# The inverse of steps 0 and 1 from products on TensorE, and groups of four from step 2 on, in a DeltaNet and MLP kernel

## Chip, cores and metric

One core of a Trainium2 chip. The metric is the device time of one execution in microseconds (us); the median of four executions is quoted (of seven for the kernel before). A "span" is the time of the one profiled execution from its first to its last record; it is 1.7 us below the run's own time in the runs before and after.

## The reference

A DeltaNet recurrence on 4 batches, 8 heads, 768 tokens and 48 features, then an MLP with a hard-swish on the 3072 x 384 result.

```python
k_n = k / (norm(k) + 1e-6)
for t in range(S):
    y[t]  = q[t] @ state
    state = state + beta[t] * outer(k_n[t], v[t] - k_n[t] @ state)
x = y as (B*S, H*D)                 # 3072 x 384
h = x @ w_in                        # 384 -> 2048
out = (h * clip(h + 3, 0, 6) / 6) @ w_out
```

`w_in` and `w_out` come as 64-bit floats and are converted to FP32 on the chip, in 16 pieces of 768 KB.

## The kernel before

The sequence is cut into 24 steps of 32 tokens. In a step, all heads of all batches are worked at once, and the recurrence inside the step becomes the inverse of a unit triangular 32x32 matrix for each of 32 heads and batches. `prep` makes k, q (transposed) and the matrix L of a step; `inverse` inverts L for four steps at once on VectorE; `chain` carries the state; `up` and `down` are the MLP.

```python
def prep(t, dma):                   # cut
    kb  = kf * inv                  # GpSimd
    mb  = beta * mask               # GpSimd
    bkb = kb * beta                 # GpSimd
    yield
    KQ  = transposes of kb, qb      # TensorE pt, ScalarE
    sc  = KQ products               # TensorE
    LB  = sc * mb                   # VectorE
    l_dram[g][i] <- L               # DMA

def inverse(g, dma, back):          # cut
    A <- l_dram[g]                  # 4 steps x 8 heads x 4 batches on 128 partitions
    for j in range(1, C - 1):       # 30 steps, each waits for the one before
        pr = A[:, j, j+1:] * A[:, 0:j, j]
        A[:, 0:j, j+1:] -= pr
        yield
    x_dram[g] <- A                  # DMA
    LB <- x_dram[g]                 # DMA, 4 of them

def convert():                      # cut: 5 instructions on VectorE, 1 on ScalarE per piece

for t in range(CB, N):              # cut: the main loop, 16 MLP units beside each chain
    ch = chain(t)
    for u in range(16):
        ...                         # a part of the chain, of a prep
        take(conv, 2)               # two of the five parts of a conversion
        take(units)
        take(fill, 1 + (u % 2 == 0))    # norms and inverse of later groups
```

The order of every engine's queue is written by hand in the program. (A few names below are short for those of the kernel: `kf` is raw k, `inv` the inverse of its norm, `R` and `Z` are steps of the chain on VectorE and ScalarE.)

## Time and profile before

| | kernel before |
|---|---|
| time, median of 7 executions (third batch) | 779.2 us (777.5 to 780.9) |
| span of the profiled execution | 777.2 us |
| first pz (chain of step 0) | 84.6 us |
| first ph (MLP) | 106.3 us |
| ks of step 4, of step 5, of step 6 | 155.4, 203.6, 231.9 us |
| granted TensorE clock, mean | 0.953 |

pz, ks, py and su are the products of the chain of a step, ph and po those of the MLP, pt and sc those of prep; g is VectorE's part of the hard-swish. "ks of step n" is the place where step n begins.

### The profile page before, as it was taken

Reading aid. Unit: us, or ns where it says so; the run is one execution under the profiler, and the core shown is the slowest. Engines: PE = TensorE matmul, PEld = TensorE weight load, DVE = VectorE, ACT = ScalarE, POOL = GpSimd, SP = SyncE. Lnnn points to the kernel's source line nnn. Section 1 sums busy time; section 2 is a strip of 40 time slices with the busy share of each in tenths; the row PEclk is TensorE's granted clock in tenths of the full one; section 3 lists DMA queues with packets and bytes.
Section 4 is the critical chain, followed back from the end, with each engine's and each line's share of the span. In section 5 each row is a group of like instructions: output and inputs, shape, how many; then the busy total and the mean of one; then the engine's idle time right before and its main releaser. Section 6 shows DMA issues by size and latency. Waiting matters only on the chain.

```text
span 777.2 us, 24923 instructions
## 1 busy us (share of the span) xinstructions
PE 677.8 (87%) x11208; PEld 500.1 (64%) x11208; DVE 356.2 (46%) x868; ACT 178.8 (23%) x354; POOL 92.0 (12%) x139
## 2 busy tenths in 40 slices
PE   1441587558799999999999999999999999999997
PEld 1330465446576776876876867867868768677674
DVE  6269859968527731247711367511464213021020
ACT  1211221222321231321322311313213113122120
POOL 4451021003004002012011040020000000000000
PEclk9995569889999999999999999999999999999999
DMA  5771750356311131330142501311103010000000
GB/s 101 184 148 48 168 115 32 116 133 187 70 39 50 23 77 35 73 65 17 44 67 45 90 29 25 66 26 30 48 12 82 6 30 3 13 13 0 21 1 20
DMA packets 140139, 45.77 MB, mean 59 GB/s; under 512 B 130272, under 2 KB 133344, under 8 KB 140032
## 3 DMA queue, kind: packets, MB, share of 16 engines
q1 hardware_dynamic: 131312, 42.23, 23.9%
q10 hardware_dynamic: 8720, 1.93, 1.3%
q8 instruction: 88, 1.44, 0.8%
q14 instruction: 19, 0.16, 0.1%
HBM read 33.13 MB, written 11.01 MB: 57 GB/s over the span
## 4 chain that ended last, share of the span: by engine, by line
PE 76%; DVE 12%; issue 3%; DMA 3%; POOL 3%; SPq 1%; ACT 1%; POOLq 0%; DVEq 0%; ACTq 0%
PE po L480 32%; PE ph L459 30%; DVE A L323 3%; DVE pr L319 3%; PE pz L371 2%; PE py L371 2%; PE su L428 2%; PE sc L287 2%; PE pt L274 2%; PE ks L361 2%; PE py L361 2%; DMA kf<-in_k_dram 1%; DMA d<-in_moe_w_in_dram 1%; DVE e L184 1%; DVE m L180 1%
## 5 line engine op out<-in xcount | busy, mean ns | idle before, releaser
L459 PE MATMUL ph<-xT,w_in 128*128 128x256 f32 x1152 | 273.8, 390 | 18.1 <-DVE w_in L189 10.2
L480 PE MATMUL po<-w_out,g 128*128 128x384 f32 x768 | 265.1, 494 | 4.0 <-DVE w_out L189 4.0
L459 PEld LDWEIGHTS ph<-xT,w_in 128*128 128x128 f32 x1152 | 216.5, 193 | 52.0 <-DVE w_in L189 10.6
L480 PEld LDWEIGHTS po<-w_out,g 128*128 128x128 f32 x768 | 141.6, 191 | 90.5 <-issue 5.6
L468 DVE SCALAR_TENSOR_TENSOR g<-t,ph 128x256 f32<-128x256 f32 x192 | 80.5, 419 | 188.6 <-ACT t L464 188.3
L464 ACT ACTIVATE t<-ph,halves 128x256 f32<-128x256 f32 x192 | 90.9, 474 | 194.1 <-PE ph L459 183.0
L323 DVE TENSOR_TENSOR A<-A,pr 128x30 f32<-128x30 f32 (+9 forms) x180 | 68.0, 378 | 6.2
L319 DVE TENSOR_TENSOR pr<-A 128x30 f32<-128x30 f32 (+9 forms) x180 | 66.8, 371 | 4.3
L436 DVE TENSOR_TENSOR state<-state,su 128x384 f32<-128x384 f32 x46 | 23.3, 547 | 67.9 <-PE su L428 67.9
L277 ACT ACTIVATE KQ<-pt 128x512 f32<-128x512 f32 x48 | 28.3, 595 | 83.6 <-PE pt L274 80.5
L287 PE MATMUL sc<-KQ 64*32 64x64 f32 x1536 | 23.1, 255 | 27.6 <-ACT KQ L277 27.6
L274 PE MATMUL pt<-ident,kb 128*128 128x128 f32 x96 | 18.1, 320 | 32.9 <-POOL kb L252 32.9
L293 DVE TENSOR_TENSOR LB<-sc,mb 128x512 f32<-128x512 f32 x24 | 16.5, 688 | 61.9 <-PE sc L287 58.4
L259 POOL TENSOR_TENSOR mb<-beta_tok,mask 128x256 f32<-128x256 f32 x48 | 32.0, 687 | 82.8 <-DVE LB L293 82.8
L252 POOL TENSOR_TENSOR kb<-kf,inv 128x384 f32<-128x384 f32 x24 | 20.7, 863 | 160.7 <-PE pt L274 131.7
L287 PEld LDWEIGHTS sc<-KQ 64*32 64x32 f32 x1536 | 18.8, 120 | 31.4 <-ACT KQ L277 30.3
L210 POOL TENSOR_TENSOR sq<-kf 128x384 f32<-128x384 f32 x21 | 17.4, 827 | 182.5 <-DMA kf<-in_k_dram 104.3
L274 PEld LDWEIGHTS pt<-ident,kb 128*128 128x128 f32 x96 | 13.4, 163 | 37.9 <-POOL kb L252 34.0
L486 ACT ACTIVATE o<-po 128x384 f32<-128x384 f32 x24 | 11.8, 491 | 111.5 <-PE po L480 111.5
L170 ACT ACTIVATE e<-e,rebias 128x768 uint32<-128x768 uint32 x16 | 15.0, 936 | 83.8 <-DVE e L169 83.7
L387 DVE TENSOR_TENSOR R<-vf,ks 128x384 f32<-128x384 f32 x23 | 12.7, 550 | 37.2 <-PE ks L361 37.2
L371 PEld LDWEIGHTS py<-Z,LB 32*32 32x32 f32 x1536 | 19.1, 109 | 13.7 <-issue 11.8
(56 smaller groups left out, 397.6 us busy)
## 6 DMA issues: line engine op xcount, KB each, us to landing
d<-in_moe_w_in_dram SPq DMA_DIRECT2D x8, 768.0 KB, 6.0
d<-in_moe_w_out_dram SPq DMA_DIRECT2D x8, 768.0 KB, 5.7
kf<-in_k_dram SPq DMA_DIRECT2D x96, 48.0 KB, 2.5
vf<-in_v_dram SPq DMA_DIRECT2D x96, 48.0 KB, 2.2
out_dram<-o SPq DMA_DIRECT2D x96, 48.0 KB, 1.6
qb<-in_q_dram SPq DMA_DIRECT2D x80, 48.0 KB, 2.4
x_dram<-A SPq DMA_DIRECT2D x6, 512.0 KB, 2.9
LB<-x_dram SPq DMA_DIRECT2D x24, 128.0 KB, 2.9
```

Source lines behind the costliest of these rows:

```text
L259: nc.gpsimd.tensor_tensor(out=mb[:, e], in0=beta_tok[:, t, e:H:2].unsqueeze(2).unsqueeze(3).to_broadcast([P, NP, 2, C]), in1=mask2[:].unsq ...
L274: nc.tensor.transpose(pt[:, p, :], src[:, 2 * p : 2 * p + 2].rearrange("p e w -> p (e w)"), ident[:])
L277: nc.scalar.activation(out=KQ[:, :, j, :], in_=pt[:], func=ACTF.Copy)
L287: nc.tensor.matmul(scv[rows(b), e, p], lhsT=KQ[r, p, 0, rows(b)], rhs=KQ[r, p, :, rows(b)], start=True, stop=True,)
L319: nc.vector.tensor_tensor(out=pv, in0=A[:, j, j + 1 :].unsqueeze(1).to_broadcast([128, j, n]), in1=A[:, 0:j, j].unsqueeze(2).to_broadcast( ...
L323: nc.vector.tensor_tensor(out=A[:, 0:j, j + 1 :], in0=A[:, 0:j, j + 1 :], in1=pv, op=ALU.subtract)
L361: nc.tensor.matmul(ph[rows(b), e, D * p : D * p + D], lhsT=KQ[r, p, j, rows(b)], rhs=state[r, b, p, :], start=(p == 0), stop=True, skip_gr ...
L371: nc.tensor.matmul(place(h, b), lhsT=m(h)[rows(b)], rhs=z[rows(b), D * h : D * h + D], start=start, stop=True, skip_group_check=True, tile ...
L459: nc.tensor.matmul(ph[:], lhsT=w_in[:, s, f * 128 : (f + 1) * 128], rhs=xT[:, s, :], start=(s == 0), stop=(s == NKT - 1),)
L464: nc.scalar.activation(out=t1[:], in_=ph[:], func=ACTF.Relu, bias=half, scale=1.0 / 6.0)
L468: nc.vector.scalar_tensor_tensor(out=g[:], in0=t1[:], scalar=1.0, in1=ph[:], op0=ALU.min, op1=ALU.mult)
L480: nc.tensor.matmul(po[:], lhsT=gs[blk, f][:, c * P : (c + 1) * P], rhs=w_out[:, f, :], start=(f == 0), stop=(f == NFC - 1),)
```

## The change

Steps 0 and 1 should not wait for the serial inverse and its way through DRAM. They become a group of their own, whose inverse comes from six rounds of 32x32 products on TensorE per step, with transposes on VectorE between them. The serial inverse then serves groups of steps 2 to 5, 6 to 9 and so on, the last with two steps. The order of the first steps is written anew around this, k and raw weights get separate buffers, and bkb is made later.

```diff
+    NG = 1 - (CB - N) // GS
+    def group(t):
+        return (0, t) if t < CB else ((t - CB) // GS + 1, (t - CB) % GS)
 ...
-                kfs[g] = stage.tile([P, GS, H, D], FP32, name="kf", tag="d", bufs=3)
+                kfs[g] = stage.tile([P, GS, H, D], FP32, name="kf", bufs=2)
 ...
+    def product(t, pool):                      # cut
+        V = L's 8x8 diagonal blocks ; F = L - V ; Y = eye - V      (VectorE)
+        def times(rhs):
+            for h in range(H):
+                for b in range(B):
+                    nc.tensor.matmul(ps[rows(b), 0:n, w], lhsT=T[rows(b), w],
+                                     rhs=rhs[rows(b), :, w], ...)
+        ps = times(V)  ; T = transpose(ps) ; V = copy(ps)          (VectorE, ScalarE)
+        ps = times(V, Y) ; ...                                     (six rounds in all)
 ...
-            inv = inverse(0, nc.scalar, nc.sync)
+            inv = inverse(1, nc.scalar, nc.sync)
 ...
-            if i == 2 and t > CB:
+            if i == 2:
                 drain(fill)
-                fill = chained(norms(g + 2, ...), inverse(g + 1, ...))
+                fill = chained(norms_of(g + 2), inverse_of(g + 1))
```

With the new grouping `i == 2` is true at step 4 (before: step 6), so the inverse of the second group starts there.

More of the change, by code (lines that the diff above doesn't have):

```diff
@@ L47 @@
     GS = 4
-    assert N % GS == 0 and GS * B * H == 128
+    assert GS * B * H == 128
     NKT = DM // 128
@@ L53 @@
     TB = CB * P
-    assert N % CB == 0
+    assert N % CB == 0 and CB <= GS
     const = ctx.enter_context(tc.tile_pool(name="const", bufs=1))
@@ L66, in rows, with size, first @@
         return slice(C * b, C * b + C)
+    NG = 1 - (CB - N) // GS
+    def group(t):
+        return (0, t) if t < CB else ((t - CB) // GS + 1, (t - CB) % GS)
+    def size(g):
+        return CB if g == 0 else min(GS, N - first(g))
+    def first(g):
+        return 0 if g == 0 else CB + (g - 1) * GS
     NKB, NQB, NBKB = 2, 4, 8
@@ L78, in load_k @@
     def load_k(t):
-        g, i = divmod(t, GS)
         if t < N:
+            g, i = group(t)
             if i == 0:
-                kfs[g] = stage.tile([P, GS, H, D], FP32, name="kf", tag="d", bufs=3)
+                kfs[g] = stage.tile([P, GS, H, D], FP32, name="kf", bufs=2)
             for b in range(B):
@@ L117 @@
             )
+    G = 8
+    eye = const.tile([P, C], FP32, name="eye")
+    nc.vector.tensor_reduce(
+        out=eye[:], in_=ident[:].rearrange("p (b c) -> p c b", b=B), axis=AX.X, op=ALU.add
+    )
+    blocks = const.tile([P, C // G], FP32, name="blocks")
+    nc.vector.tensor_reduce(
+        out=blocks[:], in_=eye[:].rearrange("p (n c) -> p n c", c=G), axis=AX.X, op=ALU.add
+    )
     halves = const.tile([128, 2], FP32, name="halves")
@@ L155, in load_w @@
             return
-        raws[i] = pool.tile([128, dst.shape[1], dst.shape[2], 2], U32, name="d", tag="d", bufs=3)
+        raws[i] = pool.tile([128, dst.shape[1], dst.shape[2], 2], U32, name="d", tag="d", bufs=2)
         nc.sync.dma_start(
@@ L193, in convert @@
             done[0] = i + 1
-            if i + 2 not in raws and i + 2 > 4:
+            if i > 1:
                 load_w(i + 2)
@@ L240, in norms @@
         for i in range(n):
-            invs[g * GS + i0 + i] = inv[:, i, :]
+            invs[first(g) + i0 + i] = inv[:, i, :]
         yield
@@ L248, in prep @@
     def prep(t, dma):
-        g, i = divmod(t, GS)
+        g, i = group(t)
         kb, qb, bkb = kbufs[t % NKB], qbufs[t % NQB], bkbufs[t % NBKB]
@@ L264, in prep @@
             )
-        nc.gpsimd.tensor_tensor(
-            out=bkb[:, :, 0:D], in0=kb[:, :, 0:D],
-            in1=bt.unsqueeze(2).to_broadcast([P, H, D]), op=ALU.mult,
-        )
         yield
@@ L278, in prep @@
             if j == 1:
-                load_q(t + NQB)
+                load_q(t + NQB, dma if t < CB else nc.sync)
             yield
@@ L296, in prep @@
         )
-        if i == 0:
-            l_dram[g] = scratch.tile([GS, H, P, C], FP32, name=f"l_dram{g}")
-            x_dram[g] = scratch.tile([GS, H, P, C], FP32, name=f"x_dram{g}")
-        dma.dma_start(
-            out=l_dram[g][i].rearrange("h p c -> p h c"),
-            in_=LB[:].rearrange("p e a j w -> p (e a) j w")[:, :, 0, :],
-        )
+        nc.gpsimd.tensor_tensor(
+            out=bkb[:, :, 0:D], in0=kb[:, :, 0:D],
+            in1=bt.unsqueeze(2).to_broadcast([P, H, D]), op=ALU.mult,
+        )
@@ L304, in prep, with plus @@
+        if g > 0:
+            if i == 0:
+                l_dram[g] = scratch.tile([size(g), H, P, C], FP32, name=f"l_dram{g}")
+                x_dram[g] = scratch.tile([size(g), H, P, C], FP32, name=f"x_dram{g}")
+            dma.dma_start(
+                out=l_dram[g][i].rearrange("h p c -> p h c"),
+                in_=LB[:].rearrange("p e a j w -> p (e a) j w")[:, :, 0, :],
+            )
         KQs[t], LBs[t] = KQ, LB
         yield
+    def product(t, pool):
+        assert G == 8 and C == 4 * G
+        LT = LBs[t][:].rearrange("p e a j w -> p (e a) j w")[:, :, 0, :]
+        by = "p (h w) -> p h w"
+        VY = pool.tile([P, 2, H * C], FP32, name="VY", bufs=CB)
+        V, Y = VY[:, 0, :], VY[:, 1, :]
+        T = pool.tile([P, H * C], FP32, name="VT", bufs=CB)
+        F = pool.tile([P, H * C], FP32, name="F", bufs=CB)
+        def times(rhs):
+            n = rhs.shape[1]
+            ps = psM.tile([P, 2, H * C], FP32, name="pi", tag="pm")
+            for h in range(H):
+                w = slice(C * h, C * h + C)
+                for b in range(B):
+                    nc.tensor.matmul(
+                        ps[rows(b), 0:n, w], lhsT=T[rows(b), w], rhs=rhs[rows(b), :, w],
+                        start=True, stop=True, skip_group_check=True,
+                        tile_position=(C * b, C * b),
+                    )
+            return ps
+        def plus(ps):
+            nc.vector.tensor_tensor(out=Y, in0=Y, in1=ps, op=ALU.add)
+        nc.vector.tensor_tensor(
+            out=V.rearrange("p (h n w) -> p h n w", h=H, w=G),
+            in0=LT.rearrange("p h (n w) -> p h n w", w=G),
+            in1=blocks[:].unsqueeze(1).unsqueeze(3).to_broadcast([P, H, C // G, G]),
+            op=ALU.mult,
+        )
+        nc.vector.transpose(out=T[:], in_=V)
+        nc.vector.tensor_tensor(
+            out=F[:].rearrange(by, w=C), in0=LT, in1=V.rearrange(by, w=C), op=ALU.subtract
+        )
+        nc.vector.tensor_tensor(
+            out=Y.rearrange(by, w=C), in0=eye[:].unsqueeze(1).to_broadcast([P, H, C]),
+            in1=V.rearrange(by, w=C), op=ALU.subtract,
+        )
+        yield
+        ps = times(VY[:, 0:1, :])
+        nc.vector.transpose(out=T[:], in_=ps[:, 0, :])
+        nc.scalar.activation(out=V, in_=ps[:, 0, :], func=ACTF.Copy)
+        yield
+        ps = times(VY[:])
+        nc.vector.transpose(out=T[:], in_=ps[:, 0, :])
+        plus(ps[:, 1, :])
+        yield
+        ps = times(VY[:, 1:2, :])
+        plus(ps[:, 0, :])
+        nc.vector.transpose(out=T[:], in_=Y)
+        yield
+        ps = times(F[:].unsqueeze(1))
+        nc.vector.transpose(out=T[:], in_=ps[:, 0, :])
+        nc.scalar.activation(out=V, in_=ps[:, 0, :], func=ACTF.Copy)
+        yield
+        ps = times(VY[:])
+        nc.vector.transpose(out=T[:], in_=ps[:, 0, :])
+        nc.vector.tensor_tensor(out=Y, in0=Y, in1=ps[:, 1, :], op=ALU.subtract)
+        yield
+        ps = times(VY[:, 1:2, :])
+        nc.vector.scalar_tensor_tensor(
+            out=LT, in0=Y.rearrange(by, w=C), scalar=-1.0,
+            in1=ps[:, 0, :].rearrange(by, w=C), op0=ALU.mult, op1=ALU.subtract,
+        )
+        yield
@@ L307, in inverse @@
     def inverse(g, dma, back):
-        A = work.tile([128, C, C], FP32, name="A", bufs=1)
+        n = size(g) * H * B
+        At = work.tile([128, C, C], FP32, name="A", bufs=1)
+        A = At[0:n]
         dma.dma_start(
-            out=A[:].rearrange("p c i -> p (c i)"),
+            out=A.rearrange("p c i -> p (c i)"),
             in_=l_dram[g][:].rearrange("t h (b c) i -> (t h b) (c i)", b=B),
@@ L315, in inverse @@
         for j in range(1, C - 1):
-            n = C - 1 - j
+            w = C - 1 - j
             pr = work.tile([128, C * C // 4 - C // 2], FP32, name="pr", bufs=1)
-            pv = pr[:, 0 : j * n].rearrange("p (c i) -> p c i", c=j)
+            pv = pr[0:n, 0 : j * w].rearrange("p (c i) -> p c i", c=j)
             nc.vector.tensor_tensor(
-                out=pv, in0=A[:, j, j + 1 :].unsqueeze(1).to_broadcast([128, j, n]),
-                in1=A[:, 0:j, j].unsqueeze(2).to_broadcast([128, j, n]), op=ALU.mult,
+                out=pv, in0=A[:, j, j + 1 :].unsqueeze(1).to_broadcast([n, j, w]),
+                in1=A[:, 0:j, j].unsqueeze(2).to_broadcast([n, j, w]), op=ALU.mult,
             )
@@ L326, in inverse @@
             yield
-        nc.vector.memset(A[:].rearrange("p c i -> p (c i)")[:, 0 : C * C : C + 1], -1.0)
+        nc.vector.memset(A.rearrange("p c i -> p (c i)")[:, 0 : C * C : C + 1], -1.0)
         back.dma_start(
             out=x_dram[g][:].rearrange("t h (b c) i -> (t h b) (c i)", b=B),
-            in_=A[:].rearrange("p c i -> p (c i)"),
+            in_=A.rearrange("p c i -> p (c i)"),
         )
-        for i in range(GS):
-            LBv = LBs[g * GS + i][:].rearrange("p e a j w -> p (e a) j w")
+        for i in range(size(g)):
+            LBv = LBs[first(g) + i][:].rearrange("p e a j w -> p (e a) j w")
             back.dma_start(out=LBv[:, :, 0, :], in_=x_dram[g][i].rearrange("h p c -> p h c"))
@@ L537, in prep_of, with load_group, norms_of, inverse_of @@
         return preps[t]
+    def load_group(g):
+        if g < NG:
+            for i in range(size(g)):
+                load_k(first(g) + i)
+    def norms_of(g):
+        return norms(g, 0, size(g)) if g < NG else iter(())
+    def inverse_of(g):
+        return inverse(g, nc.sync, nc.sync) if g < NG else iter(())
     with tc.manual_schedule():
-        with tc.tile_pool(name="early", bufs=3) as early:
-            for t in range(GS):
+        with tc.tile_pool(name="early", bufs=2) as early:
+            NE = CB + GS
+            for t in range(NE):
@@ L542 @@
                 load_k(t)
-                if t < 2:
+                if t < NQB:
                     load_q(t, nc.scalar)
             nc.scalar.activation(out=half, in_=halves[:, 0:1], func=ACTF.Copy)
-            for t in range(GS):
-                load_k(GS + t)
-            for i in range(3):
+            for i in range(2):
                 load_w(i, early)
-            drain(norms(0, 0, 1))
-            first = [prep(t, nc.scalar) for t in range(GS)]
-            take(first[0], 3)
-            load_q(2, nc.scalar)
@@ L554 @@
-            drain(norms(0, 1, GS - 1))
-            take(first[1])
-            take(first[0])
-            for t in range(1, GS):
-                if t + 1 < GS:
-                    take(first[t + 1])
-                take(first[t], 2)
-                if t == 1:
-                    load_q(3, nc.scalar)
-                if t == 3:
-                    take(conv, 3)
-                take(first[t])
-            load_v(0)
-            load_v(1)
+            for t in range(CB):
+                load_v(t)
@@ new lines @@
+            load_w(2)
+            drain(norms(0, 0, CB))
+            ps = [prep(t, nc.scalar) for t in range(NE)]
+            n1 = [norms(1, i, 2) for i in range(0, GS, 2)]
+            xs = []
+            take(ps[0])
+            take(ps[1])
+            take(ps[0], 2)
+            take(n1[0], 2)
+            for t in range(CB):
+                take(ps[t])
+                xs.append(product(t, early))
+                take(xs[t])
+                if t == 0:
+                    drain(n1[0])
+                    take(ps[1], 2)
+                take(ps[CB + t])
@@ new lines @@
+            load_group(2)
+            take(xs[0])
+            take(xs[1])
+            for n in range(CB, NE, 2):
+                take(ps[n], 2)
+                if n == CB:
+                    take(n1[1], 2)
+                take(ps[n])
+                if n + 2 < NE:
+                    drain(n1[1])
+                    take(ps[n + 2])
+                take(ps[n + 1], 3)
+                if n + 3 < NE:
+                    take(ps[n + 3])
+                take(xs[0])
+                take(xs[1])
@@ L568 @@
             load_w(3)
-            inv = inverse(0, nc.scalar, nc.sync)
+            inv = inverse(1, nc.scalar, nc.sync)
             take(inv)
-            drain(norms(1, 0, GS))
-            need(1)
-            for t in range(2):
-                take(prep_of(GS + t), 3)
-            take(prep_of(GS))
-            take(inv, 10)
-            take(prep_of(GS + 1))
-            load_w(4)
-            take(inv, 10)
-            take(conv)
-            take(prep_of(GS + 2), 2)
-            drain(inv)
@@ L583 @@
-            take(conv, 2)
-            take(prep_of(GS + 3), 2)
-            take(conv, 2)
-            for t in range(2, GS):
-                take(prep_of(GS + t), 2)
-                take(conv, 2)
-            for t in range(CB):
-                load_v(t + 2)
-                for part, _ in enumerate(chain(t)):
-                    take(conv, 1 + part % 2)
-            for n in range(GS):
-                load_k(2 * GS + n)
-            need(3)
+            for n in range(4):
+                for x in xs:
+                    take(conv, 2 if n < 2 else 1)
+                    if n >= 2:
+                        take(inv)
+                    take(x)
@@ L596 @@
+            n2 = norms_of(2)
+            for t in range(CB):
+                load_v(CB + t)
+                for _ in chain(t):
+                    take(conv)
+                    take(n2 if t else inv)
+                    take(inv)
         mlp.append(ctx.enter_context(tc.tile_pool(name="mlp", bufs=2)))
         units = mlp_units()
-        fill = chained(norms(2, 0, GS), inverse(1, nc.sync, nc.sync))
-        for t in range(CB, N):
-            g, i = divmod(t, GS)
+        fill = chained(inv, n2)
@@ new lines, in unit @@
+        def unit(n):
+            need(min(NWI, n // 2 + 2))
+            take(units)
+        load_v(CB + 2)
+        ch = chain(CB)
+        for n in range(4):
+            take(fill, 4)
+            unit(n)
+        take(ch)
+        for n in range(4, 7):
+            take(fill, 4)
+            unit(n)
+        drain(fill)
+        take(prep_of(NE))
+        take(ch)
+        take(prep_of(NE))
+        take(prep_of(NE + 1))
+        unit(7)
+        take(prep_of(NE))
+        unit(8)
+        take(ch)
@@ L601 @@
+        take(prep_of(NE))
+        take(prep_of(NE + 2))
+        take(prep_of(NE + 1))
+        unit(9)
+        take(prep_of(NE + 1))
+        take(ch)
+        take(prep_of(NE + 2))
+        take(prep_of(NE + 1))
+        drain(ch)
+        take(prep_of(NE + 2))
+        for t in range(CB + 1, N):
+            g, i = group(t)
             load_v(t + 2)
-            if i == 1 and (g + 2) * GS < N:
-                for n in range(GS):
-                    load_k((g + 2) * GS + n)
-            if i == 2 and t > CB:
+            if i == 1:
+                load_group(g + 2)
+            if i == 2:
@@ L606 @@
                 drain(fill)
-                fill = chained(
-                    norms(g + 2, 0, GS) if (g + 2) * GS < N else iter(()),
-                    inverse(g + 1, nc.sync, nc.sync) if (g + 1) * GS < N else iter(()),
-                )
+                fill = chained(norms_of(g + 2), inverse_of(g + 1))
             now = [prep_of(t + GS + i), prep_of(t + GS + i + 1)] if i < 2 else None
@@ L614 @@
             later = prep_of(t + 1 + GS + j) if j < 2 else iter(())
-            early = t < GS
+            early = t == CB + 1
             plan = {
@@ L631 @@
                     plan[u]()
-                if early and u % 2:
+                if early:
+                    if u in (1, 3, 5, 8, 11, 14):
+                        unit(10 + (1, 3, 5, 8, 11, 14).index(u))
                     continue
-                if early:
-                    need(min(NWI, ((t - CB) * NU + u) // 4 + 2))
-                else:
-                    take(conv, 2)
-                if early:
-                    take(fill, 3)
+                take(conv, 2)
                 take(units)
-                if not early:
-                    take(fill, 1 + (u % 2 == 0))
+                take(fill, 1 + (u % 2 == 0))
             drain(ch)
```

## The prediction

> **What bounds the kernel now.** I read the slices first, then the table of busy time by stretch, then the timelines of TensorE and VectorE, then the chain that ended last.
>
> ```profile
> PE   1441587558799999999999999999999999999997
> DVE  6269859968527731247711367511464213021020
> ```
>
> Each digit is 19.4 us. TensorE is full from the 12th slice to the end; in the first eleven it is not. By stretch (columns: stretch, length, busy us of PE, PEld, DVE, ACT, POOL, then granted clock, DMA share, GB/s):
>
> ```profile
> 60.00:80.00 20.00, 2.23 (x68) 1.66 (x68) 18.62 (x48) 2.39 (x4) 2.34 (x3) 0.50 0.25 73
> 120.00:140.00 20.00, 13.34 (x292) 10.45 (x292) 19.00 (x48) 2.54 (x6) 0.00 (x0) 0.91 0.12 42
> 180.00:200.00 20.00, 14.86 (x239) 10.31 (x226) 17.93 (x27) 6.22 (x11) 4.05 (x3) 1.00 0.46 133
> 300.00:400.00 100.00, 100.00 (x1748) 74.81 (x1747) 47.15 (x124) 26.36 (x54) 11.33 (x16) 1.00 0.25 51
> ```
>
> So up to about 205 us VectorE (weight conversion, inverses) is the limit, and from then on TensorE alone. After 205 us nothing is to be gained by this change; it must move the point at which TensorE becomes full. The landmarks on TensorE's and VectorE's timelines:
>
> ```profile
> 51.89 0.18 DVE L319 TENSOR_TENSOR pr<-A 128x30 f32<-128x30 f32 x1
> 77.34 0.21 DVE L323 TENSOR_TENSOR A<-A,pr 128x30 f32<-128x30 f32 x1
> ```
> ```profile
> 84.57 1.50 PE L371 MATMUL pz<-vf,LB 32*32 32x48 f32 x64
> 106.30 4.39 PE L459 MATMUL ph<-xT,w_in 128*128 128x256 f32 x12 [1.09 <-ACT xT L418]
> 160.68 4.49 PE L480 MATMUL po<-w_out,g 128*128 128x384 f32 x8 [3.95 <-DVE w_out L189]
> 203.55 0.95 PE L361 MATMUL ks<-state,KQ 64*32 64x48 f32 x60
> ```
>
> The serial inverse of the first group runs from 51.9 to 77.5 us; its way through DRAM ends at 84.6, when step 0 begins; the first MLP product comes at 106.3. The same table of TensorE instructions puts the first product of step 4's chain at 155.35 and that of step 5 at 203.55. Steps 5 to 8 then take 109.15 us (203.55 to 312.70), 27.3 each. In the chain that ended last, PE has 76% and DVE 12%, mostly L323 and L319, the inverse, and the conversions.
>
> **What the Trainium skill says.** "TensorE: Matmul & The Clock Gate", section "What's actually happening": the array's clock is halved until it has been busy for some 3.4 us, and falls back after idling. The trace agrees: 0.50 granted at 60 to 80 us, and 12 records of ph took 4.39 us at 106.3 and 2.86 at 111.4. So products in gaps cost up to twice their warm time. "DMA: Bandwidth & Descriptors", section "Anatomy of one DMA": a fixed cost of about 2 us, mostly the receipt of the last write. Here the LB reads from x_dram take 2.9 us from issue to landing, so the two trips cost about 7 us (77.64 to 84.57). "GPSIMD Engine Reference", section "Specifications": SBUF interfaces are shared with VectorE where an instruction has two SBUF inputs. The trace agrees: the 128x58 inverse step took 0.57 and 0.75 us beside GpSimd work at 53 us, 0.22 alone at 77. "VectorE: DVE Perf Modes", section "The three transpose paths": VectorE transposes 32x32 blocks only, which is all that the new product code wants; here 128x768 took 0.98 us, so I put 128x256 at 0.4 (estimate).
>
> **The change part by part.**
>
> (1) Products. Each of steps 0 and 1 gets six rounds of 32x32 products of 64 records. pz has the same count, 1.50 us cold and 0.88 warm; so 12 rounds are about 12 to 16 us of TensorE, all in a stretch in which it idles. On VectorE each step costs some 13 instructions of 128x256; g of that size takes 0.41, so 5.4 us a step, 10.7 in both.
>
> (2) Inverses. The number of serial inverses does not fall: six before (180 = 6 x 30), and now groups 1 to 6, the last of two steps only but as long on VectorE. At 22.5 us each (68.0+66.8 over 6) none is removed; each is moved. When step 4 begins, the kernel before had done two of them; the new one has done one and the products: 45 - 22.5 - 10.7 = 12 us less on VectorE.
>
> (3) The start, followed instruction by instruction. k of two steps lands by 9.6 us; with both in one set of norms inv is ready at 13.6 (before: 9.5). kb, pt, KQ, sc, as before 9 us from kb to LB, put LB of step 0 at about 21. VectorE then alternates between norms of 13 small instructions (2.7 us), LB, and product stages, and TensorE's order puts two preps between every two rounds: rounds at about 28, 38, 48 us. After LB of step 5 (47 us) only products and two conversions (3.9 us each) follow: rounds four to six from 50 to 60. X of step 0 is in place at about 60 us, of step 1 at 62, against 84.6 before. Saved: 24 us.
>
> (4) Steps 0 and 1. Before, 21.7 us from pz to the first ph. Now conversions, norms and 13 inverse steps of group 1 stand in VectorE's queue between their instructions; I count 20 us of VectorE from 63 to 83. First ph at about 83.5, saved 23.
>
> (5) Inverse 1 then has 13 steps of some 0.65 us and four g left: it ends near 98.5, and with 7 us of trips step 2's pz runs at 105.5. Steps 2 and 3 have 12 us or so of ping-pong each, with preps 6 to 9 and w_in 4 to 7 beside them; the loads for the last two are issued only when conversions 4 and 5 are done. Step 4 begins at about 134 instead of 155.35: saved 21.
>
> (6) Step 4 is where something is given back. It converts all of w_out (8 x 3.9 = 31 us), and now norms (5 us) and 15 steps of inverse 2 (12 us) are put beside them, where before there was no inverse. With g (3), state and R (1.6) that is 53 us of VectorE; before it was 37 in a stage of 48 us. But the stage before also waited for a w_out load and for the trip of the inverse in front of it, 8 us on TensorE, which now lies in steps 2 and 3. I take 53 plus 3 for the first w_out load behind 16 k loads in the queue, minus 5 for the part that TensorE need not await: 51 instead of 48. Step 5 begins at 185, saved 18.5.
>
> (7) The rest. From step 5 to the end the kernel before takes 777.2 - 203.55 = 573.7 us of full TensorE. The new one has the same to do, and the transposes of prep 10 (0.9 us). Sum: 185 + 573.7 + 0.9 = 759.6; the run is about as much above its span as rounding, so I say 759 us, 2.5% faster.
>
> **The rivals.** First: VectorE is the bound all the way to step 5, so total VectorE work counts and not when step 0 begins. By step 5 the new kernel has done about 11 us more for products and 12 for half an inverse, less half of one: level or worse, and what is saved at 84 us is given back in step 4. For it: 19.0 of 20 us busy at 120 to 140. Against it: VectorE had over 50 us idle in the first 205, 14 of them at 20 to 40 us, which can be filled. It would give 772 to 778. Second: the longer start. Six k loads, four q loads, two norms and two preps between rounds may put X of step 0 at 70 instead of 60, since each step of that chain is a wait between engines with a cold array; then the end is near 767. Third: step 4 does not stretch, because its conversions wait for loads anyway (4.55 us before at 169.0) and the inverse fills those waits; and TensorE, less often idle, is warm sooner. Then step 4 takes 44 to 46, and the end is 752 to 754. A slowdown by over 2% would need the whole start to be later, and the order gives no reason for it.
>
> **Range and chances.** The saving is 24 us at step 0, and the two largest doubts are some 8 us each in the start and in step 4; they are nearly independent, so about 12 both ways: 748 to 773. The limit for over 2% is 763.0, close above my value. I give 0.6 to faster, 0.38 to same, 0.02 to slower.
>
> **What would show it.** In the changed profile: first pz at 57 to 65 us (step 3); first ph at 80 to 88 (step 4); ks of step 4 at 128 to 140 (5); ks of step 4 to ks of step 5 some 51 us with VectorE over 90% busy (6); from there to the end 573 to 576 us (7). If the first pz is as early as I say and the end is not, step 4 took it; if the last stretch is longer than 576, TensorE did not stay full, and the new groups bring a wait that I haven't seen, such as LB of group 2 coming late for step 6.

## More of the kernel before

The next view is the table of busy time by stretch of the kernel before, for three stages: first ph to step 4, step 4, step 5. Columns: stretch, length, then busy us and number of instructions of TensorE, its weight loads, VectorE, ScalarE and GpSimd, then granted clock, share of the DMA engines, GB/s.

```profile
106.30:155.35 49.05, 35.96 (x623) 28.50 (x623) 43.96 (x110) 11.99 (x25) 8.83 (x12) 0.86 0.27 79
155.35:203.55 48.20, 33.82 (x548) 23.70 (x547) 37.27 (x53) 13.93 (x24) 7.77 (x7) 0.91 0.54 140
203.55:231.87 28.32, 28.32 (x540) 21.14 (x540) 6.21 (x13) 7.45 (x15) 0.83 (x1) 0.97 0.29 54
```

VectorE is busy for 44 of 49 us in the first stage and 37 of 48 in the second; in the third TensorE is busy all the time, and nearly so from there to the end (541.0 of 545.3 us).

## The result

768.5 us (766.1 to 769.9, 4 executions), against 779.1 us of the kernel before in the same rounds. The ratio is 0.9864, with a 95% interval of 0.9833 to 0.9896. A ratio here is the mean time of one kernel's runs over that of the other's runs of the same rounds, so it is not quite the ratio of the medians. The same kernel in a later batch (the control below) gave 767.6 us and 0.9845. The change gains 1.4 to 1.6%: within 2%, and about half of what was predicted.

| | before | after | gained so far |
|---|---|---|---|
| first pz | 84.6 | 56.6 | 28.0 |
| first ph | 106.3 | 77.1 | 29.2 |
| ks of step 4 | 155.4 | 134.1 | 21.3 |
| ks of step 5 | 203.6 | 182.8 | 20.8 |
| ks of step 6 | 231.9 | 216.3 | 15.5 |
| end of the span | 777.2 | 764.4 | 12.8 |

These are places in one profile of each kernel. The early ones vary between runs of the same code: four profiles of kernels that are alike up to step 4 (this one, the control, e1 and e2) put the first pz at 56.6, 58.2, 58.1 and 58.7 us and ks of step 4 at 134.1, 133.7, 136.2 and 134.0. A difference of 2 us at these places in single profiles says little.

The slices of TensorE in the changed kernel's page, whose digits are 19.1 us each, show the earlier work in the first ten slices:

```profile
PE   2666778757899999999999999999999999999997
```

These lines of the changed kernel's timeline of TensorE answer to the landmarks shown of before. The bracket at the end is the idle time ahead of the line and what ended it.

```profile
56.59 0.61 PE L471 MATMUL pz<-vf,LB 32*32 32x48 f32 x34 [0.68 <-DVE LB L399]
77.14 7.60 PE L559 MATMUL ph<-xT,w_in 128*128 128x256 f32 x24 [0.58 <-ACT xT L518]
98.37 1.35 PE L471 MATMUL pz<-R,LB 32*32 32x48 f32 x64 [4.77 <-DMA LB<-x_dram]
139.53 4.51 PE L580 MATMUL po<-w_out,g 128*128 128x384 f32 x8 [4.06 <-DVE w_out L212]
163.10 0.88 PE L517 MATMUL yt<-ident,y 128*128 128x128 f32 x3 [5.61 <-DVE g L568]
182.79 0.95 PE L461 MATMUL ks<-state,KQ 64*32 64x48 f32 x60
193.20 0.88 PE L471 MATMUL pz<-R,LB 32*32 32x48 f32 x64 [3.49 <-DVE R L487]
```

The way through DRAM has not gone: it now stands before step 2 (98.37). In steps 4 and 5 TensorE waits for g and R, both VectorE's, and, as before the change, for the first w_out. The busy time by stretch of the changed kernel, for the same three stages:

```profile
77.14:134.09 56.95, 44.80 (x1031) 36.42 (x1031) 41.91 (x94) 17.35 (x33) 14.43 (x18) 0.87 0.57 118
134.09:182.79 48.70, 31.09 (x404) 20.50 (x404) 41.07 (x80) 10.34 (x17) 10.72 (x11) 0.87 0.44 134
182.79:216.34 33.55, 28.53 (x412) 20.64 (x412) 23.29 (x61) 8.54 (x17) 0.83 (x1) 0.93 0.14 28
```

The first stage is 8 us longer than before, with VectorE idle for 15 us of it; TensorE has 8.8 us more work in it (44.8 us against 36.0) and is idle for about as long (12.2 us against 13.1). Step 4 is as long as before, but VectorE has 41 us to do in it instead of 37. Step 5 is 5 us longer, and in it TensorE is no longer full: 28.5 of 33.6 us, where VectorE has 23 us instead of 6. This is what the backlog looks like on VectorE's timeline; the inverse of group 2 (L419, L423), the last conversion (L207, L212), g and R in one queue:

```profile
189.65 0.95 DVE L207 SCALAR_TENSOR_TENSOR e<-d,e 128x768 uint32<-128x768 uint32 x1
190.63 0.96 DVE L212 SCALAR_TENSOR_TENSOR w_out<-m,e 128x768 f32<-128x768 f32 x1
191.51 0.41 DVE L568 SCALAR_TENSOR_TENSOR g<-t,ph 128x256 f32<-128x256 f32 x1
191.84 0.40 DVE L419 TENSOR_TENSOR pr<-A 128x240 f32<-128x240 f32 x1
192.28 0.41 DVE L423 TENSOR_TENSOR A<-A,pr 128x240 f32<-128x240 f32 x1
192.60 0.55 DVE L487 TENSOR_TENSOR R<-vf,ks 128x384 f32<-128x384 f32 x1
```

There is no idle bracket in these lines. R of step 5, for which pz waits at 193.20, is the last of them.

TensorE's busy and idle time, from the tables by stretch of both kernels, tells what became of the 28.0 us at the first pz:

| stretch | busy before | busy after | idle before | idle after |
|---|---|---|---|---|
| start to first pz | 24.2 | 30.1 | 60.4 | 26.5 |
| first pz to first ph | 14.5 | 13.1 | 7.2 | 7.4 |
| first ph to step 4 | 36.0 | 44.8 | 13.1 | 12.2 |
| steps 4 and 5 | 62.1 | 59.6 | 14.4 | 22.6 |
| step 6 to the end | 541.0 | 543.5 | 4.3 | 4.6 |

Of the 15.2 us that are lost after the first pz, 7.4 are work and 7.8 idle time. Of the work 4.9 us is the preps' (rows pt and sc after the first pz: 38.2 us against 33.3), and it is put off, not new: the kernel before had the products of eight preps behind it at its first ph, the changed one those of six. So that part of the early start was never a gain. Between first ph and step 4 the same rows are 9.4 us instead of 1.1, which is why that stage is longer although TensorE is idle no more in it. The idle time lies in steps 4 and 5.

From step 6 to the end the changed kernel takes 548.1 us and the kernel before 545.3. Of its preps, half of one and the whole of another are still to do at step 6 that the kernel before has behind it there: rows pt and sc are 27.6 us from there on, against 24.7.

### The profile page after: what moved, and what is told of

Same layout as the page of the kernel before. It is cut to its first block, busy times and chain, and to the rows that moved or that the text cites. A ratio compares the mean times of both kernels' runs of the same rounds, so it can differ in the third digit from the quotient of the medians.

```text
span 764.4 us, 26515 instructions
## 1 busy us (share of the span) xinstructions
PE 691.1 (90%) x11976; PEld 511.6 (67%) x11976; DVE 362.1 (47%) x907; ACT 180.2 (24%) x358; POOL 94.7 (12%) x141
## 4 chain that ended last, share of the span: by engine, by line
PE 77%; DVE 11%; DMA 5%; issue 4%; SPq 1%; ACT 1%; POOL 0%; ACTq 0%; DVEq 0%; POOLq 0%
PE po L580 32%; PE ph L559 30%; PE pt L293 2%; PE pz L471 2%; PE sc L306 2%; PE py L471 2%; DVE A L423 2%; PE su L528 2%; DMA qb<-in_q_dram 2%; DVE pr L419 2%; PE ks L461 2%; PE py L461 1%; DVE e L207 1%; DVE m L203 1%; PE yt L517 1%
## 5 line engine op out<-in xcount | busy, mean ns | idle before, releaser
L559 PEld LDWEIGHTS ph<-xT,w_in 128*128 128x128 f32 x1152 | 216.8, 194 | 51.7 <-DVE g L568 13.2
L423 DVE TENSOR_TENSOR A<-A,pr 128x30 f32<-128x30 f32 (+19 forms) x180 | 65.8, 366 | 6.2
L419 DVE TENSOR_TENSOR pr<-A 128x30 f32<-128x30 f32 (+19 forms) x180 | 63.8, 355 | 5.8 <-DMA A<-l_dram 2.1
L233 POOL TENSOR_TENSOR sq<-kf 128x384 f32<-128x384 f32 x23 | 20.2, 877 | 188.2 <-DVE ss L236 86.4
L471 PEld LDWEIGHTS pz<-R,LB 32*32 32x32 f32 x1472 | 18.8, 111 | 18.8 <-issue 9.0
L471 PE MATMUL pz<-R,LB 32*32 32x48 f32 x1472 | 22.0, 211 | 9.3 <-DMA LB<-x_dram 4.8
L471 PEld LDWEIGHTS py<-Z,LB 32*32 32x32 f32 x1536 | 19.1, 109 | 10.9 <-issue 9.2
```

The lines of the kernel that those rows point to most:

```text
L419: nc.vector.tensor_tensor(out=pv, in0=A[:, j, j + 1 :].unsqueeze(1).to_broadcast([n, j, w]), in1=A[:, 0:j, j].unsqueeze(2).to_broadcast([n ...
L423: nc.vector.tensor_tensor(out=A[:, 0:j, j + 1 :], in0=A[:, 0:j, j + 1 :], in1=pv, op=ALU.subtract)
L471: nc.tensor.matmul(place(h, b), lhsT=m(h)[rows(b)], rhs=z[rows(b), D * h : D * h + D], start=start, stop=True, skip_group_check=True, tile ...
L559: nc.tensor.matmul(ph[:], lhsT=w_in[:, s, f * 128 : (f + 1) * 128], rhs=xT[:, s, :], start=(s == 0), stop=(s == NKT - 1),)
```

## The experiments

Theory A: what the early start gains is given back because VectorE is the bound in steps 4 and 5, where the change has put an inverse beside the conversion of w_out. Rivals, numbered by their letters in the expectations: the loads and the transfer queue set step 4 (B), the new buffers are part of the gain (C), the products cost nothing (D), crowded conversions cost the same without the change (E).

Twelve runs were made, one of them the control. They came in batches of four (e1 to e4), four (control, e5 to e7), three (e8 to e10) and one (e11); the runs of a batch share those of the kernel before in it, and across batches I compare the ratios.

### e1: without the inverse of group 2

```diff
-                fill = chained(norms_of(g + 2), inverse_of(g + 1))
+                fill = chained(norms_of(g + 2), inverse_of(g + 1) if g > 1 else iter(()))
```

> The changed kernel without the serial inverse of group 2 (steps 6 to 9), which now lies beside the conversion of w_out in steps 4 and 5; the result is wrong on purpose. Theory A (what was won at the start is given back because VectorE is the bound in steps 4 and 5): step 4, 48.7 us in the changed kernel, falls to 42 to 44, step 5 from 33.5 to 26, and the run by about 13 us, to 753 to 758. Rival B (step 4 is as long as the loads of w_out and the transfer queue make it): at most 3 us less, 765 to 769.

755.9 us, ratio 0.9690 (0.9671 to 0.9709). Its output is wrong, which doesn't matter for the time. Against the changed kernel's 0.9845 to 0.9864 this is 12 to 14 us less. Steps 4 and 5 of this run:

```profile
136.22:178.56 42.34, 29.85 (x404) 20.43 (x404) 37.26 (x61) 10.33 (x17) 12.86 (x11) 0.88 0.47 142
178.56:205.88 27.32, 26.50 (x412) 19.44 (x411) 9.87 (x19) 8.52 (x17) 0.83 (x1) 1.00 0.06 15
```

Step 4 lost 6.4 us and step 5 lost 6.2; the conversions and their loads are all still there. B falls. The inverse of group 2 where it stands costs about as much as the whole change gains. This run says what the instructions cost, not that they could be saved: the inverse is needed, and before the change it stood in steps 6 and 7, where TensorE was busy nearly all the time. What it cost there was not measured.

### e2: one conversion part per unit instead of two

```diff
-                take(conv, 2)
+                take(conv)
```

> The changed kernel with one conversion step per MLP unit from step 4 on instead of two, so that the last conversions move from step 4 into step 5 (what is needed is still converted before its use). The work on VectorE is the same. Theory A: VectorE is the bound in step 4, so step 4 loses about 6 us and step 5 gains at most 3: 762 to 766. Rival B: loads are later too, no gain: 767 to 770.

760.7 us, ratio 0.9756 (0.9733 to 0.9779), correct. It is 7 to 8 us faster than the changed kernel, a little better than expected, and the fastest correct kernel here. Steps 4 and 5:

```profile
134.00:174.66 40.66, 30.59 (x405) 20.22 (x404) 33.76 (x71) 8.69 (x15) 8.88 (x11) 0.88 0.46 130
174.66:210.51 35.85, 29.66 (x413) 21.60 (x412) 29.07 (x70) 9.91 (x19) 0.83 (x1) 0.84 0.27 73
```

VectorE's work in the two steps together is nearly the same (62.8 us against 64.4), only the second of them has more of it. Step 4 is 8.0 us shorter and step 5 2.3 longer. So it matters where VectorE's work lies, not only how much there is.

### e9: the same edit on the kernel before

> The kernel before with one conversion step per MLP unit from step 4 on, the edit that took 7 us off the changed kernel. Theory A (that gain was work moved away from the inverse that the change puts into step 4): the kernel before has no inverse in step 4 and TensorE waits there for a load and a transfer, so 0 to 3 us less, 776 to 779. Rival E (conversions crowd step 4 in either kernel and the change has no part in it): 6 to 8 us less here too, 771 to 773.

775.8 us, ratio 0.9941 (0.9922 to 0.9960), 4.7 us less by the medians. That lies between the two expectations. Steps 4 and 5 of this run:

```profile
158.63:199.84 41.21, 32.35 (x549) 23.45 (x548) 28.03 (x41) 12.71 (x22) 7.46 (x7) 0.92 0.54 137
199.84:228.62 28.78, 28.20 (x541) 20.75 (x540) 15.24 (x25) 8.86 (x17) 0.82 (x1) 1.00 0.44 91
```

Step 4 took 41.2 us instead of 48.2 and step 5 28.8 instead of 28.3: together 6.5 us less, and e2 took 5.7 off the same two steps of the changed kernel (6.6 against the control's). This profile reached step 4 3.3 us later than that of the kernel before, though the edit touches nothing ahead of step 4; by the stages alone E is right. So the crowding of conversions in step 4 was there before the change, and most of what e2 gains, by the stages all of it, does not depend on the inverse.

### e3: only the buffers of the change

```diff
-                kfs[g] = stage.tile([P, GS, H, D], FP32, name="kf", tag="d", bufs=3)
+                kfs[g] = stage.tile([P, GS, H, D], FP32, name="kf", bufs=2)
-        raws[i] = pool.tile([...], U32, name="d", tag="d", bufs=3)
+        raws[i] = pool.tile([...], U32, name="d", tag="d", bufs=2 if pool is stage else 3)
```

> The kernel before with only the buffers of the change: k in two buffers of its own, the raw weights in two of their own, instead of three shared. Theory A: the gain comes from products and moved inverses, so nothing changes: 776 to 781. Rival C: the shared buffers held up loads (4.6 us of VectorE waiting for a w_out load at 169 us in the kernel before), and part of the gain is theirs: 770 to 774.

781.6 us, ratio 1.0023 (0.9998 to 1.0048). C falls: the separate buffers alone gain nothing. What they are worth together with the rest of the change was not tested.

### e4: the products left out

> The changed kernel with the product code of steps 0 and 1 left out (they use L where the inverse belongs; wrong on purpose). It prices the products. Theory A (VectorE's total work up to step 5 counts): 10.7 us less on VectorE and as much less waiting at the start, first pz at 45 to 50 us instead of 56.6, and the end earlier by 6 to 10 us: 758 to 763. Rival D (the products lie in idle time, and the end is set later, in steps 2 to 5): the first pz moves as much, but the end by less than 3 us.

763.6 us, ratio 0.9786 (0.9764 to 0.9808), wrong on purpose: 4.5 to 6 us less than the changed kernel by the ratios. The first pz came at 41.4 us, 15 us earlier. ks of step 4 came at 128.6 us (134.1 in the changed kernel, 133.7 in the control of the next batch), and ks of step 6 at 214.6 (216.3 and 216.8). Both theories missed, A by expecting more at the end and D by expecting less. In these profiles some 5 of the 15 us at the start are left at step 4 and some 2 at step 6: each stage passes a part on. The ends of the two profiles differ by only 1.7 us (762.7 and 764.4), less than the medians, because the profiled run of e4 was the slowest of its four and that of the changed kernel the fastest. In the profile of the changed kernel the twelve rounds are 14.2 us of busy TensorE (rows pi: 12.2 and 2.0).

### e5 and e8: when bkb is made

e5 puts this one instruction of a prep on GpSimd back to where it was, ahead of the next step's k; e8 is the kernel before with nothing but the late bkb.

```diff
+        nc.gpsimd.tensor_tensor(out=bkb[:, :, 0:D], in0=kb[:, :, 0:D], ...)   # back here
         yield
         KQ = work.tile(...)
         ...
-        nc.gpsimd.tensor_tensor(out=bkb[:, :, 0:D], in0=kb[:, :, 0:D], ...)   # from after LB
```

> The changed kernel with one small part undone: GpSimd makes bkb before it goes on to the next step's k again, instead of after LB. Theory A: in the first 20 us each step of the start waits for GpSimd, 0.83 us a step, so the first pz comes 0.8 to 2 us later and the end 0 to 2 us; within 2 us of the control. Rival: this order is what the early start rests on, and the end moves by 5 us or more.

> The kernel before with one small part of the change alone: GpSimd makes bkb after LB instead of ahead of the next step's k. Undone in the changed kernel it cost 3.8 us. Theory A (it pays only where the start is a chain from step to step, as with products): here the first inverse waits for all four LB and its way through DRAM, so 0 to 1.5 us less, 777 to 780. Rival (it is a gain of its own, a third of the change's): 3 us or more less, 774 to 776.

e5: 771.4 us, ratio 0.9896 (0.9875 to 0.9917), against 767.6 and 0.9845 (0.9817 to 0.9873) of the control in the same batch: 3.8 us more, where I expected 0 to 2. The first pz is 2.0 us later than in the control and ks of step 4 is 4.5 later. e8: 778.7 us, ratio 0.9982 (0.9967 to 0.9997), 1.8 us less by the medians, just over the 0 to 1.5 expected. So this small move is worth about 2 us alone and 4 together with the products, up to a third of what the whole change gains. That 2 us at the first pz became 4.5 at step 4 needs no explanation: against the four profiles listed under the result the first pz is 1.5 to 3.6 us later and ks of step 4 2.0 to 4.5.

### The control, and e6: no way back through DRAM for group 1

> Control: the changed kernel again, on the chip of the three other runs of this batch. Both theories: 766 to 770.

The control gave 767.6 us (765.3 to 769.2), as expected.

```diff
         nc.vector.memset(A.rearrange("p c i -> p (c i)")[:, 0 : C * C : C + 1], -1.0)
+        if g == 1:
+            yield
+            return
         back.dma_start(out=x_dram[g][:]...)
```

> The changed kernel without the transfers that bring the inverse of group 1 back through DRAM (steps 2 to 5 use L; wrong on purpose); the inverse itself is computed. Step 2's pz waits 4.8 us for that transfer in the changed kernel. Theory A: pz of step 2 comes 5 us earlier and step 4 begins 3 to 5 us earlier; of that VectorE in steps 4 and 5 lets some pass, so the end is 2 to 5 us earlier than the control. Rival: VectorE alone sets the time from step 2 on, and the end moves by less than 1 us.

766.3 us, ratio 0.9832 (0.9802 to 0.9861). Its output is wrong, which doesn't matter for the time. The interval covers the control. pz of step 2, first in the control and then in this run:

```profile
99.88 1.38 PE L471 MATMUL pz<-R,LB 32*32 32x48 f32 x57 [4.65 <-DMA LB<-x_dram]
96.43 0.88 PE L474 MATMUL pz<-R,LB 32*32 32x48 f32 x64 [0.83 <-DVE R L490]
```

It came at 96.4 us instead of 99.9, but ks of step 4 at 135.3 instead of 133.7. From first ph to step 4 this run took 56.0 us; the changed kernel, the control, e1 and e2, which all have the transfer, took 54.5 to 57.5. So my expectation that step 4 would begin 3 to 5 us earlier was wrong: the wait of 4.8 us that stands in plain sight before step 2 costs that stage nothing that can be told from the spread. At the end the runs alone (1.1 us less on average, good to some 3 us) would still allow part of the 2 to 5 us. Other waits stood in its place: in that stage of this run TensorE waited 2.2 us for a w_in conversion, 0.8 for R and 0.8 for kb, and none of these is in the changed kernel's list for the stage. That VectorE alone is the limit there, as the rival has it, does not fit either: VectorE idles 15 us in that stage of the changed kernel. What bounds steps 2 and 3 stays open; no run was made in which their preps were moved.

### e7: products for steps 0 to 3

Groups begin at step 4, so one serial inverse less is needed and none lies in step 4. The early order had to be written anew, with the third and fourth set of products beside the chain of steps 0 and 1, and 1.5 conversion parts per unit.

```diff
-        return (0, t) if t < CB else ((t - CB) // GS + 1, (t - CB) % GS)
+        return divmod(t, GS)
```

> Products for steps 0 to 3, groups of four from step 4 on: one serial inverse less in all (5), two more sets of products (10.7 us of VectorE), no way through DRAM before step 4, no serial inverse beside the conversion of w_out, and 1.5 conversion steps per unit. The early order is written anew. Theory A (what the change loses, it loses in steps 4 and 5 to the inverse put there, and in step 2 to the way back of group 1): step 4 begins at 130 to 138, steps 4 and 5 take 68 to 73 together with preps 8 to 11 in them, and the end is at 745 to 755. Rival B (step 4 is as long as loads make it, 48 us): step 6 begins near 212 and the end is at 758 to 762.

785.9 us, ratio 1.0083 (1.0061 to 1.0106), correct, and slower than both kernels (by 0.6 to 1.1% than the kernel before). Its raw weights also have fewer buffers and its first loads another order, so the run does not price the two added sets of products by themselves. Both expectations missed, because the start was lost: first pz at 69.3 us, first ph at 107.9, ks of step 4 at 163.8. Steps 4 and 5 took 74.1 us together, just above the range of A and 2.4 below the kernel before. In the start TensorE, not VectorE, lagged: from 20 us to the first ph VectorE waited 17.5 us for results of the rounds. From the list of waits of TensorE between 20 us and the first ph, for the run with four steps of products:

```profile
PE pi L352 <- issue: 15.4, 8, 4.5
PE sc L305 <- issue: 3.9, 1, 3.9
```

and for the changed kernel:

```profile
PE pi L353 <- issue: 1.5, 3, 1.1
```

The columns are us in total, number of waits, and the longest. "issue" is idle time in which the engine waited for nothing that the profile shows. Each round is 64 matmul records and 64 weight loads of 32x32. From its timeline:

```profile
62.13 0.90 PE L352 MATMUL pi<-VY,VT 32*32 32x32 f32 x74 [2.53 <-issue]
62.88 0.84 PE L352 MATMUL pi<-F,VT 32*32 32x32 f32 x53
68.27 1.22 PE L352 MATMUL pi<-F,VT 32*32 32x32 f32 x74 [4.54 <-issue]
```

The gap of 4.5 us opens inside a round, after 53 of its records. The profile also shows a queue that carries instructions in packets of 16 KB (100 packets, 1.64 MB). That instructions arrive too late, where very many small ones follow each other, would fit; but no run here tests it, and the changed kernel has such a gap of 2.9 us before a large product too (ph, between first ph and step 4). What is shown is that in this order four steps of products gave a later start than two.

### e10 and e11: attempts to do better

e10 is e2 with the transfer queue put in order and the first w_out piece converted in step 3; e11 is e2 with ScalarE's part of a conversion one part later.

```diff
# e10
-            if i == 1:
-                load_group(g + 2)
             if i == 2:
                 drain(fill)
-                fill = chained(norms_of(g + 2), inverse_of(g + 1))
+                inv = inverse_of(g + 1)
+                take(inv)
+                load_group(g + 2)
+                fill = chained(inv, norms_of(g + 2))
 ...
+                    if u >= 11:
+                        take(conv)
```
```diff
# e11
-                nc.scalar.activation(out=e[:], in_=e[:], func=ACTF.Relu, ...)
                 yield
                 nc.vector.tensor_scalar(out=m[:], ...)
+                nc.scalar.activation(out=e[:], in_=e[:], func=ACTF.Relu, ...)
```

> The changed kernel with one conversion step per unit, and with the transfer queue put in order: the k loads of a group are issued after step 3 instead of in it, the load of A for group 2 ahead of them and of the w_out loads, the first w_out block is converted in step 3, where VectorE idles, and norms come after the inverse. Theory A (steps 4 and 5 are VectorE's): work moved from step 4 into idle time of step 3 is gained, so the first po comes 3 to 4 us after ks of step 4 less, step 4 takes 35 to 38 and the end is at 753 to 757. Rival: step 3 is lengthened by as much, the end is that of the even conversion, 759 to 762.

> The changed kernel with the even conversion, and with ScalarE's part of a conversion (relu on the exponents) put one conversion step later in its queue. In the even conversion's step 5 TensorE waits 4.2 us for Z, which stands behind a relu that waits for VectorE's e. Theory A with this channel (VectorE's backlog reaches TensorE through ScalarE's queue as well as through g and R): that wait goes, Z comes at once, steps 4 and 5 lose 3 to 6 us of their 76.5, the end is at 755 to 758. Rival: VectorE's own order is the limit and g comes no earlier; 759 to 762.

e10: 762.0 us, ratio 0.9770 (0.9747 to 0.9793), no better than e2, as the rival had it. The wait before the first po fell from 4.1 to 2.7 us, but VectorE now waited 4.1 us for A in step 4, TensorE waited 4.8 us for Z behind it, and step 4 took 40.6 us as in e2. The work that was moved left a wait, not a gain.

e11: 760.9 us, ratio 0.9781 (0.9763 to 0.9799), no better either, but it tests nothing: the wait is still there. ScalarE's timeline shows the relu ahead of t and Z as before, waiting for VectorE:

```profile
187.37 0.94 ACT L198 ACTIVATE e<-e,rebias 128x768 uint32<-128x768 uint32 x1 [8.15 <-DVE e L192]
188.21 0.46 ACT L564 ACTIVATE t<-ph,halves 128x256 f32<-128x256 f32 x1
188.57 0.48 ACT L499 ACTIVATE Z<-pz 128x384 f32<-128x384 f32 x1
```

A move by one part did not take it past Z, and TensorE's wait for Z was 4.8 us (4.2 in e2). So the lines show that VectorE's backlog reaches TensorE through ScalarE's queue too; what that is worth is open.

## Why the prediction was right and where it was not

The time lies in the predicted range, 768.5 of 748 to 773. The single figure, 759, was 9.5 us too low, with 20 us forecast and 10.6 gained, and the likeliest of the three outcomes, faster by over 2% at 0.6, did not come: it is within 2%, which had 0.38. By its steps:

1. Products: right for TensorE. 14.2 us of busy TensorE, against 12 to 16.
2. Inverses: right, none was removed (180 instructions of each kind in both pages).
3. The start: right in kind, 3 us too late. First pz at 56.6 us, against 60 (58.1 to 58.7 in the three other profiles).
4. Steps 0 and 1: right, with a first ph at 77.1 against 83.5; from pz to ph it took 20.6 us, against 23.5 predicted. VectorE was busy for 19.9 us of it, as the 20 us that I counted had it.
5. Steps 2 and 3: mis-sized. From first ph to ks of step 4 I had 50.5 us, and it took 57.0. The sum for the inverse does not come out: 13 steps of 0.65 us and four g make 10 us, not the 15 that lie between 83.5 and 98.5. Yet 15.2 us is what it took (77.1 to 92.4), which is luck, and pz of step 2 followed 6.0 us later, against 7. The term that was too small is the one from that pz to step 4: 28.5 us predicted, 35.7 measured. The end of this part, 134, is right only because the first ph was 6 us early. The way of the inverse through DRAM, which I put into the sum, shows no cost in this stage when it is taken away (e6).
6. Step 4: the length is near, 48.7 us against 51, and TensorE does wait for VectorE's g; the sum behind it is not right. I had counted 53 us of VectorE in the stage, and it was 41: two of the eight conversions and 21 of the 30 steps of inverse 2 ran only in step 5. VectorE was busy for 84% of the stage, not for over 90.
7. The rest: this is the step that failed. It said that from step 5 on TensorE is full as before, with 573.7 us and 0.9 for the transposes of a prep. It was 581.6 us, 7.0 more. Step 5 took 33.6 instead of 28.3 us, and the rest 2.7 more than before. I had let the backlog end with step 4, but conversions ran on until 192 us and the inverse of group 2 until 207, and TensorE was idle for 5.0 us of step 5. e1 shows it: without that inverse step 5 takes 27.3 us. The other part is work: from step 6 on the changed kernel has the rest of one prep and the whole of another still to do, which I counted as 0.9 us and which is 2.9 by the rows pt and sc.

Step 5 thus began 2.2 us earlier than predicted and the rest took 7.0 more, which makes the measured span of 764.4 us out of the 759.6 of the sum. The prediction then made 759 of that sum, taking a run to be hardly above its span; it is 1.7 us above, so the sum means 761.3. The last 2.4 us, from the profiled run's 766.1 to the median, are spread: that run was the fastest of its four.

Of the rivals, the first (VectorE's total work gives all back) was half right: of the 29.2 us gained at the first ph 12.8 were left at the end, and steps 4 and 5 took 5.7 of what was lost. Another 4.9 us, by the rows of the preps after the first pz, is work put off, of which the prediction had 0.9 and this rival nothing. The rival was wrong in that it left out where the work lies: e2 does the same work in another place and gains 7 to 8 us (though most of that comes without the change too, as e9 shows). The second (a longer start) did not come. Nor did the third (step 4 takes 44 to 46 us, as the inverse fills waits): it took 48.7, and e1 prices the inverse at 6.4 us in it.

## What to carry to other kernels

An earlier start is worth only what the next bound lets through, and only as far as work was not merely put off to get it: count the work that the bounding engine has behind it at the same place before and after. Then count the work of the engine that is full after the part which you shorten, and look where a regrouping puts the other instructions of that engine, because a step that used to lie under a full TensorE may now lie in the one stage where it costs. When such a stage remains, spread its work over the following one before you invent more, and try that on the kernel before as well: here it gained 4.7 us there. And a wait that stands in plain sight ahead of an instruction may be worth far less than its length: take it away by itself before you plan on it.

## What the Trainium skill lacked or had wrong

- "Runtime: NRT & Kernel Launch", section "Instruction fetch mechanics", says that fetching instructions is hidden by the pace of issuing them. Whether that fails here isn't shown. But in rounds of 64 matmul records and 64 weight loads of 32x32 TensorE stood idle for nothing visible for 15.4 us in eight gaps of up to 4.5 us (e7), and the page has no figure for such rounds.
- "TensorE: Matmul & The Clock Gate", section "Wait — 56ns, not 53.3ns?", gives about 25 ns as the least time from one matmul's start to the next's; its part on packing has about 4 ns between the tiles of one pack. For a long run of small matmuls over four tile positions, as in these products, it has no figure. Here 128 records of 32x32x32 took 1.31 us at a granted clock of 1.00, 10 ns each (1.31 divided by 128), in this line of the changed kernel's timeline:

```profile
44.00 1.31 PE L353 MATMUL pi<-VY,VT 32*32 32x32 f32 x128
```
